# A new order of steps, other engines and fewer zero products ahead of the first expert's fourth chunk, in an attention and mixture-of-experts kernel

## The chip, the cores and the metric

The kernel runs on one core of a Trainium2 chip. The metric is the device time of one execution in microseconds (us). Times before are those of three runs of the unchanged kernel. One execution was also recorded by the hardware profiler; rows quoted below come from that recording. Its engines are PE (matrix products), DVE, ACT and POOL (elementwise work), and SP, which here only issues loads and stores.

## The reference

Queries, keys and values have shape (2 batches, 8 heads, 576 positions, 64). Two attentions are added: one over means of four neighbouring positions, whose output is repeated four times, and one over a band of plus or minus three positions. The sum goes through a mixture of four experts, all of them applied to every token.

```
q_d = q.reshape(B, H, Sd, 4, D).mean(axis=3)      # k_d, v_d alike
out_up = np.repeat(sm_attn(q_d, k_d, v_d), 4, axis=2)
mask = np.abs(pos[:, None] - pos[None, :]) < 4
scores = np.where(mask, scale * q @ k.T, -1e9)
out_local = softmax(scores) @ v
x = (out_up + out_local) as (1152 tokens, 512)
for e in range(4):
    h = np.maximum(x @ w1[e], 0)                  # 512 -> 1024
    out += p[:, e:e+1] * (h @ w2[e])              # 1024 -> 512
```

## The kernel before

The attention is done in four quarters, a0 to a3 (a batch and a half of its positions), and their tokens become the columns of the experts' input, in three chunks of 256 and one of 384. Products of the experts are made from a high and a low part of each operand: `whi` is a weight rounded to the engine's fast type, `wlo` the rest, and `xhi`, `xlo` the same of the tokens.

Every piece of work is a named step. A table, `ENGINE` (L20), gives the engine of steps that may run on several; a list, `ORDER` (L22 to L104), gives one global order of all steps; each engine executes its own steps in that order, whether or not a later one could go first. `WARM` (L21) gives for each step `warmN` a number of 64x64 products of zeros (`warm`, L247), whose result nobody reads. The order stands as written: the scheduler of the framework is switched to manual.

Names of steps up to the first expert: `k00n.0`, `q0n.1`, `v01n.0` and so on load half the heads of keys, queries and values of a batch and half (SP, L259); `a1q.0` to `.3` load the query rows of quarter a1 (L270); `raw101` loads a half of a weight, which is matrix 1 of expert 0, half 1 (L305), and `whi101.0`, `wlo101.0` split it in two parts (L188 or L190, and L321); `vw00` loads a window of values for the band (L291). `k01r.0` copies a loaded half to rows, `k01t.2` transposes it (PE), `k01te.2` evicts it. `k01ds.0` and `.1` sum four neighbouring keys (two additions, L399 and L400), `k01dt` transposes the result, `k01de` evicts it; `v01d.1` sums values (L480, L481). For a quarter: `a0.qt`, `a0.qte`, `a0.qd` prepare the queries (transpose, eviction, sums, L374); `a0.sc2.0` makes local scores (L547), `madd`, `max`, `sub`, `exp`, `sum`, `rec`, `norm` their softmax (max L588, sub L599, norm L618), `blk` transposes 32x32 blocks (L622), `pv` multiplies by the values (L631). `a0.ds`, `dm`, `de`, `da`, `db`, `dq`, `dt`, `dc`, `dv` are the pooled attention in four groups of heads (scores L705, maxima L720, share L750, transposition L758, values L781), and `a0.xd` its eviction. `a0.xs0` adds both for a third of the quarter (L647), `xh0` and `xl0` split the sum into `xhi` and `xlo` (L658). `clear0` and `clear1` zero the block buffers.

`m00` to `m03` are the chunks of expert 0: `m00.m0` is one of eight calls of 12 products (L814: four of `wlo` with `xhi`, four of `whi` with `xhi`, four of `whi` with `xlo`), `m00.r0` and `m00.l0` evict the high part (ACT) and the rest (DVE, L825), `m00.o01` multiplies by a quarter of the second matrix (L839; the first digit is the tile of 128 tokens, the second the part), `m00.g0` evicts (L846). Chunk m00 needs all three thirds of a0. From m03 on come the other experts, whose order is the tail of the same list.

Of the kernel before, what the change touches and what calls it, by code (L numbers as in the profile page):

```python
# [21 lines left out]
ORDER = """  # L22
    warm0 warm37 warm42 warm38 warm43 warm32 warm33 warm45 warm27 warm39 warm29 warm25 warm31 warm23 warm22 warm24
    warm21 k00n.0 k00n.1 q0n.1 q0n.0 k00r.0 q0r.0 q0r.1 warm19 warm2 k00t.0 k00t.1 a0.qt.2 warm3 a0.qt.0 a0.qt.1
    warm20 warm30 warm40 a0.qt.3 k01n.0 v01n.1 k01n.1 kstart0 v01d.1 k01ds.0 k01ds.1 v00n.1 raw101 v00n.0 v01n.0
    raw100 a1q.1 a1q.0 a1q.3 a1q.2 vw00 vw01 mask k00d.1 a0.start clear1 k00d.0 clear0 v00d.0 v00d.1 v01d.0 k00te.1
    k00te.0 k00r.1 a0.qte.0 a0.qte.2 a0.qte.1 k00t.3 warm44 k00t.2 a0.qte.3 k00te.3 k00te.2 a0.qd.0 warm18 a0.sc0.0
    a0.sc0.1 warm1 a0.sc1.0 a0.sc1.1 k01dt k01r.1 a0.qd.1 k00d.3 k01r.0 k01de a0.max1 k01t.1 warm4 k01t.0 k00d.2
    a0.max0 a0.sub1 a0.sub0 k01te.1 a0.ds0 warm16 k01t.2 a0.ds1 a0.dm0 a0.dm1 k01te.0 a0.sc2.0 warm14 warm8 k01t.3
    a0.ds2 a0.exp1 a0.exp0 a0.de0 a0.de1 a0.sum1 k01te.2 a0.da0 a0.da1 a0.db0 a0.sum0 a0.db1 a0.dq0 warm9 a0.dt0  # L30
    a0.ds3 a0.dm3 a0.dm2 a0.rec0 k01te.3 warm15 a0.sc2.1 whi100.1 a0.dc0 a0.dq1 a0.max2 a0.de2 a0.sub2 a0.dt1 warm41
    warm26 a0.norm0 a0.da2 a0.dc1 a0.db2 a0.dq2 a0.de3 a0.exp2 a0.da3 a0.db3 a0.blk0.1 a0.sum2 a0.rec1 a0.rec2
    a0.blk0.0 a0.dq3 a0.norm1 wlo100.1 a0.blk1.0 a0.blk1.1 a0.dv0 warm13 a0.dv1 a0.dt2 warm17 whi101.0 a0.dc2 warm10
    a0.dt3 a1.qt.1 warm34 warm12 a0.dv2 a0.dc3 a0.dv3 a0.pv0 warm28 whi101.1 a0.xd whi100.0 a0.xs0 a0.norm2 a1.qt.0
    a1.start a0.blk2.1 a0.blk2.0 a1.qte.0 warm7 a0.pv1 vw02 warm6 a1.qt.3 warm36 a0.pv2 warm35 a1.qt.2 raw200 a0.xs1
    raw201 praw a0.xh0 a0.xh1 a0.xl0 wlo100.0 a1.qte.1 a1.qte.3 wlo101.0 a0.xs2 whi200.1 a1.qte.2 wlo101.1 a0.xh2
    whi200.0 a1.qd.0 a0.xl1 a1.qd.1 a0.xl2 warm5 a1.sc1.1 warm11 a1.sc2.1 a1.sc2.0 a1.sc0.1 a1.ds0 m00.m0 a1.sc0.0
    m00.m2 m00.m3 a1.ds2 a1.ds1 m00.r0 a1.dm1 a1.madd2 a1.dm0 m00.l0 wlo200.1 a1.de0 a1.de1 a1.da1 a1.da0 a1.db1
    a1.dq1 wlo200.0 a1.db0 whi201.1 a1.dq0 a1.madd0 a1.dm2 a1.max2 a1.dt0 m00.m1 a1.sc1.0 a1.dc0 m00.r3 m00.r2 a1.de2
    a1.dt1 a1.ds3 m00.r1 whi201.0 m00.l3 a1.max0 a1.da2 a1.db2 a1.dm3 m00.l1 k10r.0 k10r.2 k10r.1 k10r.3 a1.dc1 m00.m4  # L40
    k10t.2 a1.dv1 m00.m6 wlo201.1 a1.madd1 a1.sub0 kstart1 a1.sub2 a1.dv0 a1.exp0 a1.de3 a1.exp2 m00.r4 m00.r6 k11r.0
    vw03 k11r.3 k11r.2 v10n.1 k11r.1 vw04 vw05 v11n.1 a1.da3 a1.dq2 a1.dt2 a1.db3 m00.l2 a1.dq3 m00.m5 a1.dc2 a1.dt3
    k10t.1 m00.o00 a1.dv2 k10t.0 m00.m7 m00.r5 a1.dc3 a1.dv3 k10te.2 m00.l4 a1.sum0 wlo201.0 a1.max1 a1.sum2 a1.sub1
    k11t.1 m00.o01 m00.l6 a1.rec0 a1.norm0 a1.blk0.0 a1.blk0.1 gate a1.rec2 a1.norm2 a1.exp1 k10te.0 m00.l5 a1.sum1
    a1.xd k10te.1 a1.pv0 k11te.1 a1.rec1 a1.blk2.1 a1.norm1 m00.r7 a1.xs0 a1.blk1.0 a1.blk1.1 a1.blk2.0 m00.l7 k11t.3
    k11t.0 m00.o10 k11t.2 k10t.3 m00.o02 k11te.0 a1.pv1 a1.pv2 k11te.2 k11te.3 k11d.1 a1.xs1 a1.xh1 k10te.3 a1.xl1
    a1.xs2 a1.xh2 a1.xh0 a1.xl0 a1.xl2 v10n.0 v10d.0 a2.start k10d.0 k10d.1 m00.o11 m00.o03 m00.o12 m00.g0 a2q.2 a2q.1
    a2q.3 a2q.0 a2.qt.0 a2.qt.1 m01.m1 a2.qt.2 a2.qt.3 m01.m0 a2.qte.1 a2.qte.2 a2.qte.0 a2.qd.0 k11d.0 v11d.1
    a2.qte.3 m01.r0 a2.qd.1 m00.o13 a2.ds0 a2.sc2.1 a2.sc0.1 a2.sc0.0 a2.sc1.0 m01.m3 m01.m2 a2.ds2 a2.ds1 m00.g1
    a2.dm1 v11n.0 a3q.3 a2.de1 a2.madd0 a2.dm0 a2.sc1.1 a2.ds3 a2.sc2.0 m01.m6 m01.l0 m01.r1 a2.de0 m01.l1 a2.da0  # L50
    a2.da1 a2.db0 a2.max0 m01.r3 a2.dq0 v10d.1 m01.r2 a2.db1 a2.dq1 a2.dm2 m01.l2 a2.dt0 m01.m4 a2.dt1 a2.madd1
    a2.max1 a2.de2 m01.l3 a2.sub1 v11d.0 vw10 a3q.2 a3q.1 a3q.0 vw11 vw12 m01.r4 a2.madd2 a2.max2 a2.dc0 m01.l4 a2.dm3
    a2.da2 a2.db2 a2.exp1 a2.sub2 a2.dc1 m01.m5 m01.r5 a2.dq2 a2.sub0 m01.l5 m01.r6 a2.de3 m01.l6 a2.sum1 a2.da3
    a2.db3 a3.start a2.dq3 m01.o10 a2.dt2 a3.qt.1 m01.o00 a2.dt3 a2.dv0 a2.dv1 m01.m7 a3.qt.2 m01.o11 m01.o12 a2.rec1
    a2.dc2 a2.exp0 a2.exp2 a2.dc3 a3.qte.1 a2.sum0 a2.rec0 a2.norm1 a2.norm0 a2.blk1.0 a3.qt.0 m01.o01 a2.dv2 a2.dv3
    m01.r7 a2.sum2 a2.blk1.1 a2.blk0.0 a2.rec2 a2.norm2 a3.qte.2 a2.xd a3.qte.0 a2.blk0.1 a2.pv0 m01.l7 a2.blk2.1
    a2.pv1 a2.xs1 a2.blk2.0 a3.qt.3 m01.o02 vw14 vw13 vw15 a3.qte.3 a2.pv2 a3.sc0.1 a3.sc1.0 a3.sc1.1 a2.xh1 a3.qd.0
    a2.xs0 a3.madd1 a2.xh0 a2.xl1 a2.xl0 a3.ds1 m01.o03 m02.m5 m02.m1 a3.ds0 m01.o13 m02.r5 a2.xs2 a3.max1 a3.qd.1
    m01.g0 a3.dm1 a3.dm0 a3.ds3 a3.sc2.0 a3.sc2.1 a3.ds2 a3.sc0.0 m02.m0 m02.m4 a3.sub1 m02.l5 m02.r1 a3.exp1 a3.de1
    m01.g1 a3.da1 a3.db1 a3.dq1 m02.r0 a3.dm2 m02.l0 a3.dt1 a3.de0 a3.madd0 a3.de2 m02.m6 m02.r6 m02.r4 a2.xh2 a3.sum1  # L60
    m02.l1 a3.max0 a3.da2 a3.madd2 a3.db2 a3.da0 a3.dq2 m02.m7 m02.m3 m02.m2 a3.dt2 a2.xl2 a3.sub0 m02.l6 m02.l4
# [1357 lines left out]
```

## Time and profile before

| | us |
|---|---|
| median of three runs | 449.85 (449.63 to 450.29) |
| the profiled execution, its own time | 449.63 |
| its span in the trace | 447.8 |
| PE busy | 439.4 |
| DVE, ACT, POOL busy | 324.5, 207.4, 107.4 |

The span goes from the first to the last recorded instruction; 1.83 us of the execution's own time lie around it. Busy time is the union of an engine's instructions; PE's is that of its products, whose ends are modelled.

### The profile page before, as it was taken

The numbers are of one execution on the slowest core, as the hardware profiler recorded it, in microseconds if no ns is written. First come the engines' busy times: TensorE is split into PE (matmuls) and PEld (weight loads), VectorE is DVE, ScalarE is ACT, GpSimd is POOL, SyncE is SP. The second block draws the span as 40 slices with busy tenths as digits, with TensorE's granted clock in tenths as the row PEclk, the third lists the DMA queues.
The fourth block names the chain that finished last, engine by engine and source line by source line (L and its number), as shares of the span: only waits on it lengthen the run. The fifth ranks groups of instructions, "written<-read, shape, count | busy, mean of one in ns | idle before, by whom it ended". The sixth has DMA issues, their size and how long they took to land.

```text
span 447.8 us, 10468 instructions
## 1 busy us (share of the span) xinstructions
PE 439.4 (98%) x4406; PEld 419.2 (94%) x4406; DVE 324.5 (72%) x574; ACT 207.4 (46%) x395; POOL 107.4 (24%) x129
## 2 busy tenths in 40 slices
...
GB/s 168 235 166 243 160 60 102 103 2 73 1 2 48 1 48 154 142 33 154 59 109 107 124 158 94 2 151 91 93 88 123 156 59 44 49 86 83 21 96 163
DMA packets 69086, 43.12 MB, mean 96 GB/s; under 512 B 27632, under 2 KB 66992, under 8 KB 69040
## 3 DMA queue, kind: packets, MB, share of 16 engines
...
q8 instruction: 34, 0.56, 0.5%
q14 instruction: 12, 0.10, 0.1%
...
## 4 chain that ended last, share of the span: by engine, by line
PE 93%; DVE 3%; DMA 1%; ACT 1%; POOL 0%; issue 0%; SPq 0%; DVEq 0%; POOLq 0%
PE ps L1069 30%; PE ps L1258 26%; PE ps L1271 4%; PE m03h L814 4%; PE m03o L839 4%; PE m01h L814 3%; PE m00h L814 3%; PE m02o L839 3%; PE m02h L814 3%; PE m01o L839 3%; PE m00o L839 3%; PE wps L247 2%; DMA q0n<-in_q_dram 1%; DVE ptb L622 1%; PE a_qt L355 1%; ACT a0pd L728 1%
## 5 line engine op out<-in xcount | busy, mean ns | idle before, releaser
L1258 PE MATMUL ps<-slot,unit 128*128 128x256 f32 x1008 | 119.9, 280 | 1.1 <-DVE unit L1178 1.1
L1258 PEld LDWEIGHTS ps<-slot,unit 128*128 128x128 f32 x1008 | 119.1, 189 | 1.3 <-DVE unit L1178 1.3
L1069 PE MATMUL ps<-xhi,slot 128*128 128x288 f32 x384 | 66.4, 295 | 0.0
L1069 PE MATMUL ps<-xc,slot 128*128 128x288 f32 x432 | 60.4, 295 | 0.0
L1069 PEld LDWEIGHTS ps<-xc,slot 128*128 128x128 f32 x432 | 58.4, 188 | 0.1
L1069 PEld LDWEIGHTS ps<-xhi,slot 128*128 128x128 f32 x384 | 56.2, 188 | 0.0
L1081 ACT ACTIVATE H<-ps 128x288 f32<-128x288 f32 x72 | 27.7, 413 | 56.7 <-PE ps L1069 56.7
L1118 POOL DMA_DIRECT2D raw<-in_moe_w_dram x15 | 19.5, 1331 | 137.6 <-DVE slot L1124 83.3
L1085 DVE TENSOR_TENSOR H<-H,ps 128x288 f32<-128x288 f32 x72 | 29.8, 450 | 20.6 <-PE ps L1069 20.4
L188 ACT CAST slot<-raw 128x1024 fp32r<-128x1024 f32 (+1 forms) x33 | 41.8, 1280 | 0.5 <-DVE raw L1017 0.4
L1023 DVE TENSOR_TENSOR slot<-raw,slot 128x1792 fp32r<-128x1792 f32 x12 | 24.3, 2023 | 23.6 <-PE ps L1069 20.9
L1069 PE MATMUL ps<-xlo,slot 128*128 128x288 f32 x192 | 41.1, 295 | 0.0
L1173 ACT ACTIVATE unit<-H 128x1024 fp32r<-128x1024 f32 x18 | 19.1, 1063 | 28.8 <-PE ps L1258 17.3
L1069 PEld LDWEIGHTS ps<-xlo,slot 128*128 128x128 f32 x192 | 30.7, 188 | 0.0
L1156 DVE SCALAR_TENSOR_TENSOR H<-H 128x1024 f32<-128x1024 f32 (+1 forms) x18 | 28.1, 1576 | 3.5 <-ACT H L1083 3.2
L1169 ACT ACTIVATE unit<-H 128x512 fp32r<-128x512 f32 (+1 forms) x24 | 20.0, 844 | 23.0 <-DVE H L1085 13.4
L1182 DVE SCALAR_TENSOR_TENSOR unit<-H,unit 128x1024 fp32r<-128x1024 f32 x18 | 22.0, 1222 | 7.1 <-ACT unit L1173 7.0
L1124 DVE TENSOR_TENSOR slot<-raw,slot 128x1024 fp32r<-128x1024 f32 x21 | 25.3, 1219 | 2.4 <-ACT slot L188 2.4
L622 DVE STREAM_TRANSPOSE ptb<-pmb 32x256 f32<-32x256 f32 x48 | 20.8, 433 | 5.1 <-PE a1pv L631 2.3
L1178 DVE SCALAR_TENSOR_TENSOR unit<-H,unit 128x512 fp32r<-128x512 f32 (+1 forms) x24 | 22.6, 953 | 1.5 <-ACT unit L1169 1.5
L1280 DVE SCALAR_TENSOR_TENSOR acc<-ps,npr,acc 128x256 f32<-128x256 f32 x48 | 20.7, 477 | 3.3 <-PE ps L1258 3.3
L247 PE MATMUL wps<-wz 128*64 128x64 f32 x286 | 21.8, 234 | 1.0 <-DVE wz L196 1.0
(321 smaller groups left out, 753.8 us busy)
## 6 DMA issues: line engine op xcount, KB each, us to landing
...
```

Source lines behind the costliest of these rows:

```text
L188: nc.scalar.copy(out_, in_)
L247: nc.tensor.matmul(T["wps"][:64, :64], wz, wz, start=True, stop=True)
L622: nc.vector.transpose(ptb[t % 2][32 * j:32 * j + 32, :, :, j, :], T[f"{a}pm{t}"][32 * j:32 * j + 32, :, :, :KW])
L814: nc.tensor.matmul(ps[:, :n], w[:, d, cc:cc + P], x[:, d, n0:n0 + n], start=i == 0, stop=i == len(terms) - 1,)
L839: nc.tensor.matmul(ps[:, cs], T[f"{nm}t{f}"][:, hpart, cc:cc + P], w[:, f % 4, cs], start=f == 0 and x == 0, stop=f == KF - 1 and x == 2,)
L1023: engine(f"wo{e}{i}").tensor_tensor(w1tile(i, 1), raw1(e, i), f32(w1tile(i, 0)), ALU.subtract)
L1069: nc.tensor.matmul(bank(acc_, n, i)[:, :NH // 2], w[:, d * P:(d + 1) * P], x[:, d, n * (NH // 2):(n + 1) * (NH // 2)], start=u == 0 and fi ...
L1081: nc.scalar.mul(dst, at, -1.0)
L1085: nc.vector.tensor_tensor(dst, dst, at, ALU.add)
L1124: engine(f"bo{e}{m}").tensor_tensor(w2tile(m, 1), raw2(q), f32(w2tile(m, 0)), ALU.subtract)
L1156: nc.vector.scalar_tensor_tensor(at[o], at[x], 0.0, at[y], ALU.max, op)
L1258: nc.tensor.matmul(ps[:, t * 256:t * 256 + 256], a[:, f, t * P:t * P + P], b[:, f], start=first_ and (t, f, x) == (0, 0, 0), stop=(t, f, x ...
```

## The change

`ORDER` is new from its start to the step `endattn`, which stands behind the last step of quarter a3; from `endattn` on the list is the same word for word. `ENGINE` gives some 55 steps another engine. Those that matter ahead of chunk m00: the row copies `k00r` and `k01r` go from ACT to DVE; `k01ds.1` and `v01d.1` from POOL to DVE; `clear0`, `a0.dq1` and `a0.norm2` from DVE to POOL; `a0.dq2` from POOL to ACT; `a1.qte.0`, `a0.xh1` and `whi200.1` from DVE to ACT. Behind its start: `whi101.0` goes from ACT to DVE, `wlo101.1` and `wlo200.0` from POOL to DVE, `wlo200.1` and `wlo201.1` from DVE to POOL, and some small steps of a1 to a3 change engine in both directions. `WARM` sums to 110 products where it summed to 143; in both kernels all of them stand ahead of the first product of m00. The zeros at the edge of four value windows become a step of their own, `vw00e` and so on, on DVE or POOL.

```diff
-WARM = [8, 24, 22, 23, 9, 6, 6, 5, 4, 3, 4, 0, 1, 2, 0, 0, 0, 2, 1, 0, 0, 0, 0, 2, 0, 0, 3, 0, 1, 0, 1, 0, 2, 0, 0, 1, 2, 2, 0, 0, 2, 3, 3, 0, 1, 0]
+WARM = [4, 2, 0, 0, 3, 1, 1, 0, 5, 2, 0, 2, 7, 0, 3, 7, 0, 4, 0, 8, 2, 0, 4, 1, 4, 1, 0, 2, 5, 7, 0, 9, 0, 0, 0, 0, 0, 14, 3, 2, 2, 0, 2, 0, 0, 3]
...
     def vwin(b, i):
 
         name = f"vw{b}{i}"
+        first, last = i == 0, i == 2 * NT - 1
+        edge = [f"{name}e"] if first or last else []
+
+        def edges():
+            T[name] = a3.tile([P, H, D], F32, tag="vw", name=name)
+            engine(f"{name}e").memset(T[name][96:128] if last else T[name][0:R], 0.0)
+        if edge:
+            step(f"{name}e", "G", [], edges)
+
         def fn():
-            vw = T[name] = a3.tile([P, H, D], F32, tag="vw", name=name)
-            first, last = i == 0, i == 2 * NT - 1
-            if first:
-                nc.gpsimd.memset(vw[0:R], 0.0)
-            if last:
-                nc.gpsimd.memset(vw[96:128], 0.0)
+            if not edge:
+                T[name] = a3.tile([P, H, D], F32, tag="vw", name=name)
             for j in range(4):
...
-        step(name, "S", [], fn)
+        step(name, "S", edge, fn)
```

What the lists make of the queues is shown at three places. The first is the head of SP's queue. A row is a load, `k01n` a half of the heads of the second half of the keys, `raw_247` the weight half `raw101`, `raw_251` and `raw_463` the half `raw100`. Before:

```order
L259 DMA k00n<-in_k_dram 72x4x256 x2
L259 DMA q0n<-in_q_dram 72x4x256 x2
L259 DMA k01n<-in_k_dram 72x4x256
L259 DMA v01n<-in_v_dram 72x4x256
L259 DMA k01n<-in_k_dram 72x4x256
L259 DMA v00n<-in_v_dram 72x4x256
L305 DMA raw_247<-in_moe_w_dram 128x4x512
L259 DMA v00n<-in_v_dram 72x4x256
L259 DMA v01n<-in_v_dram 72x4x256
L305 DMA raw_251<-in_moe_w_dram 128x4x512
```

Now:

```order
L259 DMA k00n<-in_k_dram 72x4x256 x2
L259 DMA q0n<-in_q_dram 72x4x256 x2
L259 DMA k01n<-in_k_dram 72x4x256 x2
L259 DMA v01n<-in_v_dram 72x4x256
L259 DMA v00n<-in_v_dram 72x4x256
L311 DMA raw_463<-in_moe_w_dram 128x4x512
L259 DMA v01n<-in_v_dram 72x4x256
L270 DMA acc<-in_q_dram 72x8x64
L259 DMA v00n<-in_v_dram 72x4x256
```

The second half of `k01n` moved from the seventh to the sixth place, the values `v01n` behind it, and `raw101` from the ninth place to the 28th, behind the value windows.

The second place is DVE's queue ahead of the first chunk: its last rows up to `a0.xl2`, the last piece of `xlo` that m00 needs. Lines behind L286 stand six higher in the changed kernel (L653 is L647). Before:

```order
L184 TENSOR_SCALAR a1qT<-a_qt_662 128x4x72
L647 TENSOR_TENSOR a0pv_679<-a0pv_679,a0xd 128x384
L190 CAST xhi<-a0pv_679 128x4x96
L647 TENSOR_TENSOR a0pv_706<-a0pv_706,a0xd 128x384
L190 CAST whi_743<-raw_721 128x1024
L374 TENSOR_REDUCE a1qd<-a1qT 128x144
L658 TENSOR_TENSOR xlo<-a0pv_679,xhi 128x4x96
L374 TENSOR_REDUCE a1qd<-a1qT 128x144
L658 TENSOR_TENSOR xlo<-a0pv_706,xhi 128x4x96
```

Now:

```order
L653 TENSOR_TENSOR a0x_652<-a0pv_623,a0xd 128x384
L628 STREAM_TRANSPOSE ptb_92<-pmb_101 32x8x32 x4
L653 TENSOR_TENSOR a0pv_690<-a0pv_690,a0xd 128x384
L380 TENSOR_REDUCE a1qd<-a1qT 128x144
L664 TENSOR_TENSOR xlo<-a0pv_690,xhi 128x4x96
L653 TENSOR_TENSOR a0pv_753<-a0pv_753,a0xd 128x384
L380 TENSOR_REDUCE a1qd<-a1qT 128x144
L726 TENSOR_REDUCE a1dmx<-a1sd_765 72x2
L664 TENSOR_TENSOR xlo<-a0pv_753,xhi 128x4x96
```

The eviction `a1qT`, the cast `xhi` and the cast `whi` of the 1024 columns of `raw_721` are gone from this stretch (they are ACT's now); the maxima `a1dmx` of a1's pooled scores stand ahead of the last `xlo`.

The third place is PE's queue around the first product of m00 (`m00h`). Before:

```order
L631 MATMUL a0pv_706<-ptb_92,vw_688 64x96 x8
L247 MATMUL wps<-wz 64x64
L355 MATMUL a_qt_716<-ident,acc 128x72 x4
L247 MATMUL wps<-wz 64x64 x6
L547 MATMUL a1sl<-kT_231,a1qT 32x32 x64
L705 MATMUL a1sd_828<-kd_232,a1qd 72x144
L705 MATMUL a1sd_829<-kd_232,a1qd 72x144
...
L814 MATMUL m00h_834<-xhi,wlo_589 128x256 x4
L814 MATMUL m00h_834<-xhi,whi_542 128x256 x4
L814 MATMUL m00h_834<-xlo,whi_542 128x256 x4
```

Now:

```order
L247 MATMUL wps<-wz 64x64
L637 MATMUL a0pv_753<-ptb_92,vw_748 64x96 x8
L711 MATMUL a1sd_765<-kd_143,a1qd 72x144
L711 MATMUL a1sd_766<-kd_143,a1qd 72x144
...
L553 MATMUL a1sl<-kT_142,a1qT 32x32 x32
L820 MATMUL m00h_824<-xhi,wlo_740 128x256 x4
L820 MATMUL m00h_824<-xhi,whi_480 128x256 x4
L820 MATMUL m00h_824<-xlo,whi_480 128x256 x4
```

The local scores of a1 (`a1sl`, 16 products for each step) all stand ahead of m00 now, 96 of them, where 64 stood ahead and two steps of 16 behind; the transpositions `a_qt` are earlier, and no zero product stands between the last `a0pv` and m00, where seven stood.

## Rows read from the trace of the kernel before

**Rows 1.** The page: part 1, busy time; part 4, the chain by engine.

```profile
PE 439.4 (98%) x4406; PEld 419.2 (94%) x4406; DVE 324.5 (72%) x574; ACT 207.4 (46%) x395; POOL 107.4 (24%) x129
...
PE 93%; DVE 3%; DMA 1%; ACT 1%; POOL 0%; issue 0%; SPq 0%; DVEq 0%; POOLq 0%
```

**Rows 2.** Busy time by stretch: us, engines (instructions), clock, DMA share, GB/s.

```profile
0.00:42.60 42.60, 39.12 (x806) 34.80 (x806) 26.94 (x80) 23.48 (x47) 27.15 (x44) 1.00 0.82 206
42.60:140.00 97.40, 97.40 (x1275) 84.87 (x1274) 70.45 (x189) 38.35 (x118) 34.61 (x49) 1.00 0.29 61
```

**Rows 3.** The chain of waits, 40.7 to 60 us (start, us, what); timeline of PE.

```profile
40.77 1.25 PE a1sl L547 x78
...
48.68 1.47 PE m00h L814 x12
...
42.60 0.74 PE L814 MATMUL m00h<-xhi,wlo 128*128 128x256 f32 x4
```

**Rows 4.** Busy time of the zero products alone (L247), first stretch.

```profile
0.00:42.60 42.60, 21.84 (x286) 19.60 (x286) 1.00 0.82 206
```

**Rows 5.** Timeline of POOL and ACT: start, us, instruction, [idle before, releaser].

```profile
13.11 1.27 POOL L480 TENSOR_TENSOR v01n<-v01n 72x512 f32<-72x512 f32 x1 [10.82 <-DMA v01n<-in_v_dram]
...
14.76 2.00 ACT L188 COPY kr<-k01n 72x1024 f32<-72x1024 f32 x2 [0.20 <-DMA k01n<-in_k_dram]
...
21.03 0.40 ACT L188 COPY kd<-k01dt 128x288 f32<-128x288 f32 x1 [4.27 <-PE k01dt L405]
```

**Rows 6.** DVE, 20.57 to 43.00 us: busy time, then timeline.

```profile
20.57:43.00 22.43, 19.46 (x58) 1.00 0.78 206
...
20.98 0.45 DVE L382 TENSOR_REDUCE kd<-k00t 128x72 f32<-128x288 f32 x1
...
21.34 0.48 DVE L588 TENSOR_REDUCE a0mx<-a0sl 128x4 f32<-128x128 f32 x2
...
35.56 0.41 DVE L618 TENSOR_TENSOR pmb<-pmb,a0sl 128x256 f32<-128x256 f32 x1
...
37.82 0.67 DVE L184 TENSOR_SCALAR a1qT<-a_qt 128x288 f32<-128x288 f32 x1
...
39.12 0.56 DVE L190 CAST xhi<-a0pv 128x384 fp32r<-128x384 f32 x1
...
40.06 0.68 DVE L190 CAST whi<-raw 128x1024 fp32r<-128x1024 f32 x1
...
42.91 0.45 DVE L720 TENSOR_REDUCE a1dmx<-a1sd 72x2 f32<-72x288 f32 x1
```

**Rows 7.** Groups by line and form, 0 to 140 us: shapes, count, busy us, mean ns.

```profile
L321 POOL TENSOR_TENSOR wlo<-raw,whi 128x256 fp32r<-128x256 f32 x24 | 17.3, 751 | 0.1
...
L374 DVE TENSOR_REDUCE a0qd<-a0qT 128x144 f32<-128x576 f32 x2 | 1.4, 748 | 0.0
...
L618 POOL TENSOR_TENSOR pmb<-pmb,a0sr 128x256 f32<-128x256 f32 x2 | 1.4, 682 | 0.8 <-DVE a0sr L615 0.7
...
L190 DVE COPY kT<-k01t 128x288 f32<-128x288 f32 x2 | 1.3, 665 | 0.0
...
L647 DVE TENSOR_TENSOR a0pv<-a0pv,a0xd 128x384 f32<-128x384 f32 x2 | 1.1, 562 | 0.0
...
L284 POOL MEMSET vw<- 4x512 f32 x2 | 1.0, 516 | 0.0
...
L658 POOL TENSOR_TENSOR xlo<-a0x,xhi 128x384 fp32r<-128x384 f32 x1 | 1.0, 999 | 0.4 <-ACT xhi L188 0.4
```

**Rows 8.** DVE, the 28.10 us from the first expert product.

```profile
42.60:70.70 28.10, 22.07 (x61) 1.00 0.61 125
```

**Rows 9.** Timeline of SP: start and us of a pair of weight loads.

```profile
33.28 1.00 SPq L305 DMA_DIRECT2D raw<-in_moe_w_dram  x2
```

More of the change, by code (lines that the diff above doesn't have):

```diff
@@ L26 @@
[L26 to L60, printed above, removed]
@@ L61 @@
-    m02.l1 a3.max0 a3.da2 a3.madd2 a3.db2 a3.da0 a3.dq2 m02.m7 m02.m3 m02.m2 a3.dt2 a2.xl2 a3.sub0 m02.l6 m02.l4
-    a3.exp0 m02.r3 a3.rec1 m02.l3 m02.r2 a3.dc2 a3.dc1 a3.db0 a3.dm3 a3.sum0 m02.l2 m02.o00 m02.o01 a3.dq0 a3.de3
-    a3.da3 a3.db3 a3.dq3 a3.dt3 m02.o02 a3.dv2 m02.r7 a3.rec0 m02.l7 a3.dv1 m02.o10 a3.dt0 m02.o03 a3.max2 a3.sub2
-    a3.exp2 a3.norm0 a3.norm1 a3.sum2 a3.blk0.0 a3.blk0.1 a3.pv0 a3.dc3 a3.dc0 a3.rec2 a3.norm2 a3.blk1.0 a3.blk1.1
-    a3.dv0 a3.dv3 a3.blk2.0 a3.blk2.1 m02.o11 a3.pv2 a3.pv1 a3.xd a3.xs0 a3.xs1 m02.g0 a3.xs2 a3.xh1 a3.xh0 a3.xh2
@@ L101 @@
[L101 to L103 removed]
+    warm25 mask warm12 a0.start warm17 kstart0 warm29 k00n.0 k00r.0 warm31 k00t.1 k00t.0 k00te.1 k00n.1 warm45 q0n.0
+    warm19 warm9 k00r.1 k00t.2 k00te.0 q0n.1 k00t.3 k00d.0 k00d.2 warm40 k01n.1 warm28 warm42 q0r.0 k00d.1 k00d.3
@@ new lines @@
+    warm27 k01n.0 v01n.0 warm34 k01ds.0 warm39 k00te.2 q0r.1 a0.qt.2 k00te.3 a0.qt.0 v01d.0 a0.qte.2 k01r.1 a0.qt.1
+    warm15 a0.qte.0 k01ds.1 k01r.0 a0.qt.3 k01t.3 k01te.3 a0.qte.1 a0.sc0.0 a0.qd.0 a0.qte.3 a0.sc0.1 a0.max0 k01t.1
+    a0.sub0 a0.qd.1 k01t.0 k01te.0 k01te.1 k01dt k01de a0.sc1.0 a0.sc1.1 a0.ds0 a0.ds1 a0.max1 v00n.0 v00d.0 warm24
+    a0.dm0 a0.exp0 a0.sum0 a0.rec0 a0.norm0 a0.sub1 warm8 clear0 a0.de0 a0.dm1 a0.de1 k01t.2 a0.sc2.0 k01te.2 a0.da0
+    a0.sc2.1 a0.db0 a0.dq0 a0.da1 raw100 a0.max2 a0.db1 a0.dq1 a0.sub2 a0.exp1 v01n.1 a0.ds2 whi100.1 a0.ds3 a0.dm3
@@ new lines @@
+    a1.qte.0 a1.sc1.1 a1.sc1.0 wlo100.1 a0.xs1 a0.xh1 warm6 vw02 a0.pv2 a0.xl0 a1.qd.0 a1.ds0 warm7 wlo100.0 a0.xl1
+    a0.xs2 a1.sc0.0 a1.qd.1 a1.dm0 a0.xh2 a0.xl2 a1.sc2.0 raw101 k10r.3 a1.madd0 whi101.0 whi101.1 wlo101.1 m00.m2
+    m00.r2 a1.ds1 a1.dm1 m00.l2 a1.de0 a1.max0 m00.m0 a1.sub0 a1.da0 a1.db0 a1.ds2 warm21 a2.start a1.de1 m00.r0
+    m00.l0 m00.m1 k10r.0 raw200 m00.r1 a1.madd2 wlo101.0 k10r.2 a1.exp0 a1.sum0 a1.rec0 a1.dq0 a1.dm2 a1.da1 whi200.0
+    a1.db1 a1.dq1 a1.ds3 a1.de2 m00.m3 m00.l1 k11r.1 a1.dt0 k10r.1 m00.r3 m00.m4 a1.dt1 a1.dc1 a1.madd1 a1.dm3 a1.de3
```

115 lines of the change are left out of this document (72 added, 43 removed).

## The prediction

> **What bounds the kernel now.** I read the page first: PE is busy 439.4 of 447.8 us, and of the chain that ended last 93% is PE's [rows 1]. Such a share is a mean, and PE is kept busy by products of zeros too; so the next view is busy time by stretch, cut where the first product of chunk m00 starts, at 42.60 [rows 2, 3]. Behind the cut PE is busy in all of 97.40 us, and no zero product runs there any more. Ahead of it PE is busy 39.12 of 42.60 us, but 21.84 of these are zeros [rows 2, 4]. The reader is to see two regimes: up to 42.60 PE waits for attention a0 and fills the time; from there it is the bound without a gap, with a fixed amount of work, while DVE is busy 70.45 of 97.40. Since the order from the last step of a3 on is the old one, the time changes by three things alone: how much earlier m00 starts, what work goes from one side of the cut to the other, and what new waits PE gets behind it.
>
> Ahead of the cut it is DVE that paces. Its row from the maxima of a0 to the last `xlo` takes from 20.57 to 43.00, 22.43 us with 19.46 busy [rows 6]; the row starts late because the pooled keys are late. The last half of `k01` is taken up at 14.76 [rows 5]; POOL sums both halves after `v01d.1`, and the summed keys reach `kd` at 21.03, 6.3 us later [rows 5].
>
> **The start of DVE's row.** In the new order the last half of `k01` is the sixth load. The sixth load before was the half of `v01` that POOL took up at 13.11 [rows 5], so I put it there, 1.65 earlier than 14.76. Its sums are split: one half on POOL, the other, which lands earlier, on DVE. The instruction at 13.11 took 1.27, and a half sum is that and one of half its columns: 1.27 + 0.64 = 1.9 us. The pooled keys are summed at 13.1 + 1.9 = 15.0, against 21.03 for `kd` before, and their scores need not hold anybody up. From 13.1 DVE does, in its order, a row copy (0.68, as the copy of 1024 columns in [rows 6]), `k01te.3` (0.67) and both sums of a0's queries (0.75 each) [rows 7], and `max0` with `sub0` (0.48 for each pair [rows 6]): 13.1 + 0.68 + 0.67 + 1.50 + 0.96 = 16.9.
>
> **The length of DVE's row.** What follows up to `a0.xl2` is the old row with eight steps out and three in. Out, from [rows 6]: one pooled key sum 0.45; `max0` and `sub0` 0.48 each (they are in the 16.9); `norm2` 0.41 and `dq1`, taken at the same 0.41; `a1.qte.0` 0.67; `xh1` 0.56; `whi200.1` 0.68. Sum 4.14. In: the window's zeros `vw00e`, on POOL 0.52 [rows 7] and taken at that; a1's first maxima 0.45 [rows 6]; and `v01d.1`, which no row shows on DVE. Its bounds are POOL's 1.9 above, and from DVE's `xs`, 0.562 for 384 columns [rows 7], 0.562 x 768/384 = 1.12 for its 512 and 256; I take the DVE one, since engine and operation are the same. Sum 2.09. The row keeps its waits: 22.43 - 4.14 + 2.09 = 20.4, and it ends at 16.9 + 20.4 = 37.3. Before, the first product of m00 stood 0.40 ahead of that end (42.60 against 43.00), because eight products come ahead of the first that reads `xlo`. So m00 would start at 36.9 by DVE.
>
> What would keep the moved steps from being free is named here. ACT takes `a1.qte.0`, `xh1` and `whi200.1` and gives away four row copies; it is busy 23.48 of 42.60 [rows 2]. POOL takes two `clear` and shares: from 13.1 it does four half sums (7.6), six steps like `norm` (0.68 each, 4.1), two clears of 1024 columns (twice the 0.516 of a 512 memset, 2.1), eight pieces of `wlo` (0.751 each, 6.0) and one `xlo` (1.0) [rows 7]. That is 20.8, so it has `wlo100.0` by 33.9 if it never waits, 3.0 in hand. The two rows, DVE's and POOL's, end near each other, and each waits for the other's products, so I take 37.2 for the start, 5.4 earlier. The bounds: with none of DVE's 2.97 of waits 33.9 (POOL's row says the same), with twice as many 39.9.
>
> **Fewer zero products.** 33 of 143 go; one costs 21.84/143 = 0.153 us [rows 4], so PE has 33 x 0.153 = 5.0 us less ahead of m00. Were they not gone, an earlier start would not be possible; as they are, PE's work ahead of the cut is 39.12 - 5.0 + 0.6 (below) = 34.7 in 37.2 us, 2.5 idle where 3.48 were. The granted clock is 1.00, the 2.4 GHz level, in both stretches [rows 2], and by this row nothing changes in it. The Trainium skill, "TensorE: Matmul & The Clock Gate", section "HAM oscillation — how this bites in real kernels", speaks against the change: it says that a wait between groups of products can throttle the engine again, which then starts the next group at half speed. No stretch of this trace shows that; the sum goes by the row, and the rule is a rival below.
>
> **Moved over the cut.** The four calls of local scores of a1 ahead of m00 took 1.25 us, 0.31 each [rows 3]; two more now stand ahead. PE has 0.6 us less behind it: -0.6.
>
> **New waits behind the cut.** DVE gets, net of what goes both ways, some 1.8 us more behind the cut: `whi101.0` 0.68, three `norm` or `sub` of 0.41, a cast, and evictions of a1 in both directions; the two `wlo` pieces only change places with two others. 70.45 + 1.8 = 72.3 in 96.8: 24.5 idle instead of 27.0. In all that is enough, so what counts is the places. I added durations along each engine's new row from the start of m00. DVE has `wlo200.0` after 9.5 us, and PE reads it in m00.o10 at 10.8; POOL has `wlo200.1` after 11.6 (it waits for `whi200.1` on ACT), needed in m00.o01 at 14.2; DVE has m00.l7 after 26.2, needed in m00.o13 at 28.1. The same addition over DVE's old row gives 21.6 where 22.43 passed, 4% less; stretched so, 0.9 remains in hand at each of the two DVE places. That is little for rows that wait for each other. I take 0.6 lost at each, 1.2 in all; the bounds are 0 and, with the additions stretched by 15%, 0.1 at o10, 2.0 at o13 and some 0.9 behind it at a2's pooled values (`v10d.1` stands on DVE behind an eviction and a sum there): 3.0. The split of the window's zeros changes nothing else: they take a step of 0.52 out of POOL or put it there, ahead of the windows' loads, in both kernels.
>
> **The sum.** -5.4 - 0.6 + 1.2 = -4.8. The profiled execution took 449.63, so 444.8; it lies 0.22 below the median of the three runs, so **445.1** against 449.85.
>
> **Rivals.**
> - *m00 starts as DVE's row says, and nothing waits behind it*: 449.85 - 5.7 - 0.6 = 443.5. For it: PE has no wait in 97.40 us before. Against: 0.9 in hand is thin. Chance 0.10.
> - *POOL sets the start.* Its 3.0 in hand are used up when it waits 5 us for denominators and casts: start at 38.9, 449.85 - 3.7 - 0.6 + 1.2 = 446.8. Chance 0.07.
> - *DVE becomes the bound behind the cut*, up to m00.l7. In the 28.10 us after the first product it was busy 22.07, 79% [rows 8]. Waits of 3.0 to 6.9 there give 446.9 to 450.8; chance 0.12, of which 0.05 from waits of 5.1 on, within 0.2% of before. It **ends slower** if PE loses over 6.9 (5.4 + 0.6 + 0.9), when 26.2 us of DVE's row take 28.1 + 6.9 = 35.0, a share of 75%. For: DVE's steps now wait for ACT and POOL at more places. Against: 79% with fewer steps crammed in. A loss of 7.2 gives 451.1; chance 0.05.
> - *The clock falls* in a gap of PE ahead of m00 or beside it, the page's rule above. An m call takes 1.47 us [rows 3]; at 1.2 GHz it would take 2.94, and four slow calls lose 5.9: 451.0. By the granted clock of before, 1.00 throughout, I give it 0.05 (0.03 slower, 0.02 the same).
> - *`raw101` comes late.* It is the 28th load now, and DVE stops at `whi101.0`, with m00.l2 queued behind it and `wlo101.1`; PE's fourth m call waits for that. By the additions this costs from a landing at 38.9 on. The nearest row is the weight pair issued at 33.28, the 29th and 30th load of before [rows 9], whose second use stands at 40.06 [rows 6]: at worst 40.1, so 1.2 us, 446.3; the gain is gone only at 43.7. Chance 0.03, of which 0.01 slower.
> - *The forecast* keeps 0.58.
>
> **How the numbers follow.** A change under 0.2% (0.9 us) can't be told from none with these runs. Faster: 0.58 + 0.10 + 0.07 + 0.07 of DVE's case + 0.02 of the late load = 0.84. The same: 0.05 + 0.02 = 0.07. Slower: 0.05 + 0.03 + 0.01 = 0.09. The forecast's own bounds are a start at 36.2 to 38.6 with stalls of 0 to 3.0, not all at one end: 443.2 to 447.5. The range goes from 443.0 to 448.8: below lies little of the no-stall case (0.03), above what ends the same or slower (0.16).
>
> **What would show each step.** Right: m00 starts near 37 us; the summed keys reach `kd` near 16; zero products take near 17 us; the granted clock stays 1.00; PE's waits behind the start sum to 1 us, before m00.o10, m00.o13 or a2's pooled values; from the tail on every stretch is as long as before. Wrong: a start after 39 (POOL's or DVE's row waits more), waits of over 3 us on DVE or POOL behind the cut, or a granted clock under 1.00.

## The result and the profile after

The changed kernel takes 447.15 us, the median of 20 executions (441.31 to 450.03), against 449.60 for the kernel before (448.36 to 450.29, 20 executions): 2.45 us less, 0.54%. The ratio, 0.9905 with a 95% interval of 0.9879 to 0.9930 (0.95%, 4.3 us of 449.6), leaves out the seven slowest executions of the changed kernel, from 448.31 on, and none of the kernel before. On another chip, with all twelve executions of the changed kernel in it, the ratio was 0.9941 (e5), so a gain of 0.5 to 0.6% is the safer figure. The forecast was 445.1 in 443.0 to 448.8.

The spread is news: 8.7 us where the kernel before has 1.9. It goes with TensorE's granted clock. The five executions with a mean clock of 1.000 took 442.45 to 444.38 and the one with 0.999 441.31, those with 0.996 445.21 to 449.09, those with 0.992 447.91 to 449.70, the ones with 0.989 and 0.983 449.24 and 450.03.

The profiled execution took 445.98, its span is 444.1 and its mean clock 0.996. From the page, PE's busy time, the queue called instruction, and the chain by engine [rows 1]:

```profile
PE 434.0 (98%) x4340; PEld 416.0 (94%) x4340; DVE 329.6 (74%) x580; ACT 206.6 (47%) x398; POOL 101.9 (23%) x122
...
q8 instruction: 34, 0.56, 0.5%
...
PE 97%; issue 1%; DVE 1%; ACT 0%; DVEq 0%
```

Busy time of the two stretches, cut at the first products of m00 and m03 (columns as in [rows 2]), and the zero products alone:

```profile
0.00:38.91 38.91, 34.56 (x804) 30.99 (x804) 29.26 (x81) 20.23 (x47) 22.80 (x38) 0.99 0.82 208
38.91:136.42 97.51, 96.40 (x1215) 85.25 (x1209) 76.08 (x196) 40.87 (x122) 33.86 (x47) 0.98 0.34 74
```

```profile
0.00:38.91 38.91, 16.92 (x220) 15.39 (x220) 0.99 0.82 208
```

The start of m00 moved from 42.60 to 38.91 (-3.69); from there to m03 it is 97.51 where it was 97.23 (+0.28); the rest of the span is 307.68 where it was 307.97 (-0.29). Sum -3.70. The zeros take 16.92 us [rows 4], as forecast. So nearly all of the gain is the start, and it is smaller than the 5.4 of the forecast. PE's waits show why (engine, line, releaser: us, times, longest; those for the first `wz` and, far behind m03, for `unit` are left out):

```profile
PE a0pv L637 <- issue: 2.1, 1, 2.1
...
PE m01h L820 <- issue: 1.1, 1, 1.1
...
PE a0sl L553 <- issue: 0.6, 1, 0.6
PE wps L247 <- issue: 0.5, 1, 0.5
```

These four lines are new in kind: 2.1 us ahead of a product of `a0pv`, 1.1 in `m01h`, 0.6 in `a0sl`, 0.5 at a zero product, each put down to "issue", which is to say that no semaphore explains it. Ahead of m00 the list has no wait of PE for another engine once its first zero product has started: of 38.91 - 34.56 = 4.35 us idle, 1.0 lies ahead of that product and 3.2 in three of these stops. PE's timeline shows where the longest is:

```profile
34.33 0.59 PE L637 MATMUL a0pv<-ptb,vw 128*64 128x96 f32 x9
37.03 0.55 PE L637 MATMUL a0pv<-ptb,vw 128*64 128x96 f32 x7 [2.11 <-issue]
...
38.91 1.22 PE L820 MATMUL m00h<-xhi,wlo 128*128 128x256 f32 x4
...
41.64 0.74 PE L820 MATMUL m00h<-xhi,wlo 128*128 128x256 f32 x4
```

The stop lies in the middle of one step, the third `pv`, whose data were all there for its first nine records. Behind it the first call of m00 takes 2.73 us (38.91 to 41.64) instead of 1.47 [rows 3]. The clock, by stretch of PE (busy, clock, DMA share, GB/s):

```profile
34.92:37.03 2.11, 0.00 (x1) 1.00 0.96 340
38.00:39.00 1.00, 1.00 (x69) 0.71 1.00 185
39.00:41.00 2.00, 2.00 (x10) 0.50 0.94 120
41.00:42.00 1.00, 1.00 (x7) 0.58 0.91 306
```

PE did nothing for 2.11 us. Some 1.4 us after it resumed the granted clock fell to 0.50, the 1.2 GHz level: a mean of 0.71 over 38 to 39 puts the fall near 38.4, 0.58 over 41 to 42 the rise near 41.8, 3.4 us in all. What PE had executed at each stop is the count in its busy time from the start:

```profile
0.00:14.90 14.90, 13.27 (x221) 1.00 0.79 197
...
0.00:25.60 25.60, 23.50 (x474) 1.00 0.83 195
...
0.00:36.90 36.90, 32.69 (x725) 1.00 0.81 205
...
0.00:82.30 82.30, 76.94 (x1355) 0.98 0.65 153
```

221, 474, 725, 1355: the differences 253, 251 and 630 are, within one record, 2, 2 and 5 times 126. A block of 126 recorded products is 252 recorded instructions with their weight loads. The page's queue "instruction" moved 34 packets of 16 KB, and PE executed 4340 + 4340 instructions, 255 for each packet. One such packet starts between 34.25 and 34.50, just ahead of the long stop (queue: packets, MB, their time as a share of 16 engines' 0.25 us):

```profile
q8 instruction: 1, 0.02, 29.8%
```

It takes 0.298 x 16 x 0.25 = 1.19 us, so it has landed by 35.7, and PE goes on at 37.03. In the packet records of the kept traces the same holds at all 21 stops of this kind: the packet ends 1.3 to 1.7 us before PE goes on. By the same count the kernel before passed a block about as fast, 41.2 to 44.7, and did not stop. There the packet started between 42.25 and 42.50, some 1.2 us after the border; here it started some 3.5 us after (border at 30.97). The DMA engines were less loaded there from the border on, 0.71 against 1.01 (columns as in [rows 2]), before and now:

```profile
41.20:44.70 3.50, 3.50 (x147) 3.10 (x139) 2.15 (x5) 1.12 (x2) 3.50 (x6) 1.00 0.71 131
```

```profile
30.97:34.49 3.52, 3.52 (x139) 3.29 (x132) 3.38 (x8) 2.15 (x4) 3.52 (x6) 1.00 1.01 333
```

The Trainium skill, "Runtime: NRT & Kernel Launch", section "Instruction fetch mechanics", says that an engine's instructions stream in by blocks of 16 KiB, 256 instructions, the next one while the current one is executed, and that this is mostly hidden. The count agrees; hidden it is not here.

The engines that the forecast spoke of, ACT, DVE and POOL (timelines), and DVE over 28.10 us from m00's first product [rows 8]:

```profile
16.14 0.44 ACT L188 COPY kd<-k01dt 128x288 f32<-128x288 f32 x1
...
22.61 0.62 DVE L486 TENSOR_TENSOR v01n<-v01n 72x512 f32<-72x512 f32 x1
...
23.26 1.37 DVE L487 TENSOR_TENSOR vd<-v01n 72x256 f32<-72x256 f32 x1
...
37.62 0.57 DVE L653 TENSOR_TENSOR a0pv<-a0pv,a0xd 128x384 f32<-128x384 f32 x1 [2.68 <-PE a0pv L637]
...
33.11 2.78 POOL L327 TENSOR_TENSOR wlo<-raw,whi 128x256 fp32r<-128x256 f32 x4
```

```profile
38.91:67.01 28.10, 22.83 (x60) 0.95 0.48 105
```

The summed keys are in `kd` from 16.14 (21.03 before [rows 5]). `v01d.1` takes 0.62 and 1.37 on DVE beside POOL's sums, 2.0 in all where 1.12 was taken. DVE has its second `xs` at 33.12 and then waits 2.68 for the stopped PE. POOL ends `wlo100.0` at 35.9. With the 2.1 us simply taken off, m00 would start at 36.8, an estimate; the forecast took 37.2.

### The profile page after: what moved, and what is told of

The parts are those of the page before. It is cut to its first block, busy times and chain, and to the rows that moved or that the text cites. A ratio compares the mean times of both kernels' runs of the same rounds, so it can differ in the third digit from the quotient of the medians.

```text
span 444.1 us, 10352 instructions
## 1 busy us (share of the span) xinstructions
PE 434.0 (98%) x4340; PEld 416.0 (94%) x4340; DVE 329.6 (74%) x580; ACT 206.6 (47%) x398; POOL 101.9 (23%) x122
## 4 chain that ended last, share of the span: by engine, by line
PE 97%; issue 1%; DVE 1%; ACT 0%; DVEq 0%
PE ps L1075 30%; PE ps L1264 27%; PE ps L1277 4%; PE m03h L820 4%; PE m03o L845 4%; PE wps L247 3%; PE m00h L820 3%; PE m01h L820 3%; PE m02h L820 3%; PE m00o L845 3%; PE m01o L845 3%; PE m02o L845 3%; PE a_qt L361 1%; PE a0pv L637 1%; DVE slot L1130 1%
## 5 line engine op out<-in xcount | busy, mean ns | idle before, releaser
L1124 POOL DMA_DIRECT2D raw<-in_moe_w_dram x15 | 19.5, 1297 | 145.5 <-DVE slot L1130 85.2
L188 ACT CAST slot<-raw 128x1024 fp32r<-128x1024 f32 (+1 forms) x33 | 41.8, 1280 | 0.5 <-DVE raw L1023 0.4
L1017 POOL DMA_DIRECT2D raw<-in_moe_w_dram x8 | 11.8, 1532 | 36.5 <-DVE H L1091 20.7
```

The costliest lines, as they stand in the source:

```text
L188: nc.scalar.copy(out_, in_)
```

## The experiments

Theory A: PE stops at the border of a block of its own instructions when the next block has not come, because the new order packs short products (a1's scores) into one block while loads are busy; a long stop lets the clock fall. Theory B: PE waits for data. Theory C: fewer zeros as such let the clock fall. The first four runs shared a chip on which the kernel before itself took 448.41 to 460.98 in 23 executions with clocks of 0.972 to 1.00; there the verdicts rest on the profiles. On the chips of the later sets it took 448.36 to 450.51, but for one of 46 executions.

**Fewer zeros at the start (e1).**

```diff
-WARM[31] = 9
+WARM[31] = 3
```

> The changed kernel with 6 zero products fewer in its first group, ahead of 6 us; nothing else. Theory A (PE stops where a block of its own instructions, 126 recorded products long, has not come in yet, and the clock falls after a long stop): all stops move with the count. The one behind 725 recorded products leaves the middle of the third a0pv and lies 12 recorded products later, in a1sd; the block ahead of it takes some 4.5 us instead of 3.9, so the stop shrinks from 2.1 to about 1.5 us; the one behind 1355, 1.1 us in m01h, goes. Time about 444 to 445. Theory B (PE waits there for data, the loaded window or another engine): the stop stays ahead of the same product of a0pv with the same 2 us, the time stays at 446. Theory C (fewer zeros as such let the clock fall): six more gone, the clock is granted 0.996 or less, 446 or more.

447.27 us median of 6 (444.01 to 452.71), ratio 0.9864 (0.9784 to 0.9944). PE's timeline:

```profile
34.68 0.47 PE L711 MATMUL a1sd<-kd,a1qd 64*72 64x144 f32 x4
36.99 0.63 PE L711 MATMUL a1sd<-kd,a1qd 64*72 64x144 f32 x4 [1.84 <-issue]
```

The stop now lies 12 records later in the program, in `a1sd`, and the trace has 724 products ahead of it; the third `pv` runs through. It shrank from 2.11 to 1.84 (1.5 forecast), that in `m01h` is gone. m00 starts at 38.37. B falls: a wait for the window would have stayed where it was. C is not parted by this run: the mean clock is 0.996 or less in all six executions, but this chip's clock falls with the kernel before too.

**Thirty-six zeros fewer at the start (e2).**

```diff
-WARM[12], WARM[19], WARM[28], WARM[29], WARM[31] = 7, 8, 5, 7, 9
+WARM[12], WARM[19], WARM[28], WARM[29], WARM[31] = 0, 0, 0, 0, 0
```

> The changed kernel with 36 zero products fewer, all from the groups ahead of 9 us, where PE waits for loads. Theory A: the blocks' borders fall 72 recorded products later in the program, on stretches where PE runs through a block fastest: behind 671 (3.3 us for the block before it), 797 (2.9), 1301 (1.2, the local scores of a2) and 1679 (2.4, those of a3). Stops of 1.5 to 4 us at several of these counts, several falls of the clock, and a time of 449 to 456 although only idle fill was taken out. Theory B: stops at the same products as before, time 446 within 1 us. Theory C: the clock falls in the first 15 us, where the zeros are gone, and m00 starts as it did; 446 to 448.

458.59 us (6; 455.61 to 464.62), ratio 1.0142 (1.0072 to 1.0212). The counts of the expectation are those of the program's places in the old numbering; less the 72 records taken out they are 599, 725, 1229 and 1607. Timeline and counts:

```profile
36.80 0.58 PE L553 MATMUL a1sl<-kT,a1qT 64*32 64x32 f32 x44 [2.40 <-issue]
...
43.48 0.33 PE L553 MATMUL a1sl<-kT,a1qT 64*32 64x32 f32 x8 [3.13 <-issue]
...
87.70 0.53 PE L553 MATMUL a2sl<-kT,a2qT 64*32 64x32 f32 x37 [3.29 <-issue]
...
0.00:34.50 34.50, 28.56 (x598) 1.00 0.84 188
...
0.00:40.50 40.50, 32.12 (x724) 0.97 0.86 199
...
0.00:85.00 85.00, 73.05 (x1227) 0.94 0.63 142
```

Three stops of 2.4 to 3.3 us stand at 598, 724 and 1227 records, all inside local scores; none shows at 1607. The profiled execution took 455.61, that of e1 on the same chip 444.01, though only 30 more zeros at the start are gone: each of these borders now meets a run of short products. A holds at its sharpest place. Not all of the loss is theirs: with the zeros of the start gone, the eight records of transpositions from 5.75 and from 8.14 take 1.19 and 1.22 us, where the changed kernel's take 0.72 each, which A does not explain.

**Three score steps behind the first m calls (e3).**

```diff
-... a1.sc1.1 a1.sc1.0 ... a1.sc2.0 ... m00.m2 ... m00.m0 ...
+... m00.m2 ... m00.m0 a1.sc1.1 a1.sc1.0 a1.sc2.0 ...
```

> The changed kernel with three of a1's six score steps (sc1.1, sc1.0, sc2.0, 96 recorded products) moved behind the first two m calls of m00; the same work. Theory A: the block that ends at 725 recorded products is filled by longer products, takes 6 us or more, and PE has no stop ahead of m00; m00 starts near 36 instead of 38.9, the clock stays 1.00 there, time 442 to 443.5, less spread. Theory B: the stop of 2 us in the third a0pv stays, m00 starts 1.2 us earlier only by the work moved behind it, which comes back there: 446. Theory C: the clock falls as before, 446.

```profile
36.19 0.72 PE L820 MATMUL m00h<-xhi,wlo 128*128 128x256 f32 x4
```

m00 starts at 36.19, at the full clock, with no stop ahead of it, and the profiled execution, at 1.00 throughout, took 444.89, above the 442 to 443.5 of theory A: stops of 0.8 and 1.0 came at later borders, and 0.9 for DVE at the moved scores. The median of 12 is 453.48, ratio 1.0003 (0.9943 to 1.0062), on the restless chip; as a time it decides nothing.

**The kernel before with as many zeros fewer as in the change (e4).**

```diff
-WARM[1], WARM[2], WARM[3] = 24, 22, 23
+WARM[1], WARM[2], WARM[3] = 13, 11, 12
```

> The kernel before with 33 of its 143 zero products taken out of its three largest groups, as many as the change takes out; no other edit. Theory A: the zeros cost nothing by themselves, but the borders of blocks fall 66 recorded products later: one at 791, in or behind the local scores of a1, with 1.5 to 2.5 us for the block before it, so PE stops there for 2 to 4 us just ahead of m00 and the clock falls: 452 to 455. The reading of the prediction (zeros are fill, DVE paces up to m00): no change, 449 to 450, no stop. Theory C: the clock falls between 9 and 20 us, where the zeros are gone; 450 to 451. A rival to the prediction (zeros stand in the way of real work): 446 to 448.

454.22 us (12; 451.20 to 459.97), ratio 1.0044 (1.0003 to 1.0085). Clock by stretch of PE:

```profile
8.00:12.00 4.00, 3.03 (x26) 0.60 1.10 233
...
29.00:33.00 4.00, 4.00 (x45) 0.54 0.70 132
...
33.00:39.00 6.00, 6.00 (x61) 0.50 0.99 340
```

Here C has its part. PE stops 1.9 us for a load's copy ahead of 9 us and 1.4 for POOL ahead of 28, and behind each the clock is at half; m00 starts at 46.62, 4.0 later than before, with a stop at a border of only 0.8 ahead of it (2 to 4 expected by A). The zeros of the old order were not mere fill.

**The changed kernel again (e5).** No edit.

> The changed kernel unedited, beside the others of this set on one chip. Theory A (PE stops at borders of 126 recorded products when the next block of instructions has not come): stops behind 725 recorded products again, of 1 to 3 us, m00 near 38 to 39, perhaps behind 221, 473 and 1355; times that go with the granted clock, some 444 at 1.00 and 2 to 4 us more for each fall. Theory B (a wait for data): the stop may be anywhere or missing.

446.80 us (12; 444.34 to 448.30), ratio 0.9941 (0.9924 to 0.9959). The stop behind 725 records came again in the third `pv`, now of 3.6 us; m00 started at 42.11 in that profile, which took 448.21. Of 29 executions of the kernel before in this set 28 had a clock of 0.998 or more; of the 12 of the changed kernel two.

**Both helpful edits (e6).** The edit of e1, and of e3's three steps only sc1.1 and sc1.0.

> The changed kernel with both edits that helped: 6 zero products fewer in the first group, and two of a1's score steps (sc1.1, sc1.0, 64 recorded products) behind the first two m calls of m00. Theory A: no stop ahead of m00 over 0.5 us, m00 starts near 36, none behind 1355; clock 1.00; the profiled run at 441 to 442.5, its median at or under that of the changed kernel beside it. If the gain of the moved scores comes back behind m00, as it did in part with three moved: 443 to 444.

444.23 us (6; 441.41 to 445.12), ratio 0.9881 (0.9854 to 0.9908) beside the 0.9941 of e5 on the same chip. PE's timeline:

```profile
36.12 0.25 PE L553 MATMUL a1sl<-kT,a1qT 64*32 64x32 f32 x4 [0.90 <-issue]
36.31 0.74 PE L820 MATMUL m00h<-xhi,wlo 128*128 128x256 f32 x4
```

A stop of 0.9 is left, still behind 724 records, not under 0.5; m00 starts at 36.31, m03 at 132.62 (136.42), and the profiled execution took 442.19 at a clock of 1.00. Four of the six executions still had 0.995 or 0.996.

**Five steps back on DVE (e7).**

```diff
-'a0.dq1': 'G', 'a0.norm2': 'G', 'clear0': 'G', 'a1.qte.0': 'A', 'a0.xh1': 'A'
+'a0.dq1': 'V', 'a0.norm2': 'V', 'clear0': 'V', 'a1.qte.0': 'V', 'a0.xh1': 'V'
```

> The changed kernel with five steps ahead of m00 back on DVE, where the kernel before had them: dq1 and norm2 of a0, clear0, a1.qte.0 and a0.xh1, together 0.41 + 0.41 + 0.9 + 0.67 + 0.56 = 3.0 us. The prediction's reading (DVE's row sets the start of m00): the start moves from 38.9 to 39.9 to 42, since 2 of the 3 us may lie under the stop for instructions; 447 to 449. Rival (the row of PE or POOL sets it, DVE has room): start within 0.5 of 38.9, 445 to 447.

449.35 us (10; 446.98 to 450.77), ratio 0.9998 (0.9980 to 1.0016).

```profile
39.77 0.91 PE L637 MATMUL a0pv<-ptb,vw 128*64 128x96 f32 x7 [2.56 <-issue]
...
42.60 1.22 PE L820 MATMUL m00h<-xhi,wlo 128*128 128x256 f32 x4
```

The start moves by 3.69 to 42.60 for 3.0 us of steps, beyond the forecast 42. Of the 3.69, 2.29 come ahead of the stop, which begins at 37.21 instead of 34.92: PE has waits of 0.9, 0.7 and 0.6 for DVE there that the changed kernel's profile does not show. The stop is 0.45 longer and hides nothing, and behind it PE needs 2.83 us to m00 instead of 1.88, at half clock. So DVE's row had some 0.7 us of room in that profile, no more, and this relief alone, undone, takes the whole gain.

**The keys' part undone (e8).**

```diff
-'k01ds.1': 'V', 'k01r.0': 'V', 'k01r.1': 'V'
+'k01ds.1': 'G', 'k01r.0': 'A', 'k01r.1': 'A'
```

> The changed kernel with the keys' part undone: k01ds.1 back on POOL (2.0 us there for 1.1 on DVE), the row copies k01r.0 and .1 back on ACT (1.05 each for 0.69). The loads keep their new order. The prediction's reading (DVE's row paces, the pooled keys only have to come before its first maxima at 18): pooled keys 2 us later, start of m00 0 to 1 us later, 446 to 447. Rival (the early pooled keys carry the gain): start 2 us later or more, 448.

449.25 us (10; 448.27 to 452.73), ratio 1.0008 (0.9988 to 1.0028). Timeline and clock of PE:

```profile
18.82 0.50 PE L411 MATMUL k01dt<-ident,k01dp 72*128 72x72 f32 x2 [2.45 <-POOL k01dp L406]
...
18.00:25.00 7.00, 6.18 (x101) 0.51 1.01 182
...
43.30 0.75 PE L820 MATMUL m00h<-xhi,wlo 128*128 128x256 f32 x4
```

My own expectation falls, the rival's 2 us are exceeded. The sum stands behind `v01d.0` in POOL's row; PE waits 2.45 us for it in `k01dt`, the clock is 0.51 from 18 to 25 and at half again from 35.1 to 38.5, and m00 starts at 43.30, although no stop stands at 725 records here. The early keys matter because PE stands in `k01dt`: DVE then waits 3.25 us for the local scores behind it.

**One load moved (e9).** On SP, vw03 right behind raw101 (`raw101 vw03` in `ORDER`).

> The changed kernel with one load step moved on SP: the fourth value window vw03, whose buffer comes free at the first a0pv, stands right behind raw101, so the key rows k10r and the weights raw200 and raw201 are issued some 2 us later. PE's rows are untouched. Theory A2 (the block of instructions comes late because it stands behind those loads): the stop behind 725 recorded products shrinks from 2.1 to 3.6 us to under 1.5, the clock falls less, 444 to 445. Rival (the block is late because PE runs through the one ahead of it in 3.9 us, whatever the loads do): the stop stays at 2 to 3.6 us, 446 to 447.

443.80 us (4; 443.06 to 444.03), ratio 0.9877 (0.9861 to 0.9894). SP's issue of raw200 in the changed kernel, and that of the key rows and raw200 in this one, with PE's third `pv`:

```profile
30.21 1.29 SPq L311 DMA_DIRECT2D raw<-in_moe_w_dram  x1
```

```profile
33.13 1.28 SPq L270 DMA_DIRECT2D acc<-in_k_dram  x2
...
34.46 1.87 SPq L311 DMA_DIRECT2D raw<-in_moe_w_dram  x1
...
36.48 0.55 PE L637 MATMUL a0pv<-ptb,vw 128*64 128x96 f32 x7 [0.25 <-issue]
```

With raw200 issued 4.25 us later (34.46 for 30.21) the stop at the same place is 0.25 us. So whether PE has to wait for a block depends on the traffic, not only on how short the block ahead of it is. In this profile PE ran at half clock from 29.7 to 33.1, so that block also took longer (31.69 to 35.98, 4.3 us instead of 3.7). The packet parts the two: it starts between 34.00 and 34.25 here, 2.3 to 2.6 us after the border, against some 3.5 in the changed kernel. So the block came sooner, and that does not hang on PE's pace. All four executions have clocks of 0.996 or more. What lies ahead of the half clock is no long stop (timeline, then the stretch at half clock):

```profile
26.84 1.02 PE L764 MATMUL a0pdt<-ident,a0pd 72*72 72x72 f32 x8 [0.62 <-ACT a0pd L753]
```

```profile
29.71:33.12 3.41, 3.41 (x94) 0.50 0.82 226
```

**All three edits (e10).**

> The three edits together: 6 zeros fewer in the first group, two score steps of a1 behind the first m calls, vw03 ahead of the key rows. Theory A2: no stop over 0.5 us ahead of m00, clock 1.00 in most executions, 441 to 443. Rival: as with the first two edits, a stop of about 0.9 us, 442 to 445.

442.53 us (4; 441.95 to 444.07), ratio 0.9848 (0.9829 to 0.9866): a median under those of both kernels; the changed kernel itself was not run on this chip. Three of four executions ran at 1.00 (441.95 to 442.64); the profiled one, 444.07, had half clock from 29.6 to 33.1, and m00 started at 37.58 with no stop behind 724 records ahead of it.

**The keys' part alone in the kernel before (e11).** Loads `k01n.1 k01n.0 v01n.1`, k01ds.1 and k01r on DVE, k01dt behind warm1.

> The kernel before with the keys' part of the change alone: both halves of k01 are loaded ahead of the values, one half is summed on DVE, the row copies k01r are on DVE, and the transposition k01dt stands behind the 24 zeros of warm1 rather than behind two score steps; all other rows are the old ones. If the early pooled keys carry the gain (undone in the changed kernel, they cost 4.4 us up to m00): m00 starts 2 to 4 us earlier, 446 to 448. If the rest of DVE's and PE's rows sets the start: within 1 us, 449 to 450.

449.76 us (12; 449.05 to 450.58), ratio 1.0013 (1.0003 to 1.0024).

```profile
42.20 0.75 PE L814 MATMUL m00h<-xhi,wlo 128*128 128x256 f32 x4
```

m00 starts 0.4 earlier, at 42.20, and no time is won. But the edit did not make the keys early. ACT, and DVE's row copy (timelines):

```profile
19.59 0.40 ACT L188 COPY kd<-k01dt 128x288 f32<-128x288 f32 x1 [5.68 <-PE k01dt L405]
...
15.52 2.59 DVE L190 COPY kr<-k01n 72x1024 f32<-72x1024 f32 x1
```

The summed keys reach `kd` at 19.59, only 1.4 us earlier than before, since the row copy takes 2.59 us and `k01ds.1` follows it on DVE; DVE's maxima of a0 start at 20.71, where they started at 20.57. So whether keys as early as the changed kernel's (16.14) would help the old order is not tested.

## Why the prediction was right

**The start.** That DVE's row is long enough to set the start held: 3.0 us more on it move PE's arrival at the stop by 2.3 (e7). That it alone paces did not: in the changed kernel's profile PE, with its zeros, waits for no other engine ahead of m00, so the two rows are about equally long. Without the stop m00 would start at 36.8, by 36.9 for DVE and 37.2 taken. That is in part luck, for terms were off and cancelled: `v01d.1` cost 2.0 for 1.12 and the row copy `k01r.0` 1.79 for 0.68, while the row's waits were shorter. POOL's 3.0 in hand were enough. That early keys "need not hold anybody up" is true of the split as made; e8 shows that their absence does, through PE.

**The zeros.** 16.92 us against 16.8. But "by this row nothing changes in it" (the clock) failed. The same cut in the old order costs 4.0 us up to m00 by stops that let the clock fall (e4), and in the new one the mean clock was 0.996 or less in 14 of 20 executions. The rival of the falling clock, at 0.05, came true in kind: smaller in size (1.26 us in m00's first call instead of 5.9), and not in outcome. By the prediction's own list a granted clock under 1.00 is a sign of being wrong. The rule of the Trainium skill, "TensorE: Matmul & The Clock Gate", section "HAM oscillation — how this bites in real kernels", that a wait may throttle the engine, which no row of before could show, agrees with these traces in part: half clock follows the 2.11 us here, 2.45 in e8 and 1.9 and 1.4 in e4. The next products do not start at half speed here, as the rule has it, but 1.4 us pass first. No fall follows the 1.1 in `m01h` or the 0.9 of e6, and three falls (29.7 in e9, 29.6 in e10, 35.1 in e8) stand 2.8 us behind a wait of only 0.6 for ACT, which in e1 and e3 has none behind it. What decides is open.

**What failed** is the step that PE only waits for other engines. No term, no rival and no row was given to its own instructions: 2.11 us ahead of m00 and 1.1 in `m01h`. A row was there, 34 packets in the queue "instruction" on the page of before, and that a block is 126 products could have been worked out from it. That the new order runs through one in 3.7 us (30.97 to 34.67 in the trace of after) would not have been enough, since the old one did so in 3.5 without a stop; the loads at that moment had to be read too.

**New waits behind the start.** 1.2 us were taken at m00.o10 and m00.o13, up to 3.0 with a2's values: none of these stopped PE, though DVE was busy 22.83 of 28.10 us instead of 22.07. In their place came the 1.1 in `m01h` and the 1.26 of the slow clock, 2.4 in sum.

**Moved work.** Two score steps, -0.6. With +2.4 the stretch should be 97.23 + 1.8 = 99.0; it is 97.5. Some 1.5 us of PE's time are gone that no moved step accounts for: the same 144 products of the second matrix keep PE busy 36.80 us instead of 37.67, the pooled scores 3.71 instead of 4.17. e9, at the full clock behind its start (134.34 - 38.29 = 96.05, with one stop of 0.9), has them too. That PE changes less often between kinds of products is a guess; it stays open.

**The sum.** -4.8 forecast; -3.65 in the profiled execution, -4.3 by the ratio, -2.45 by the medians of all. That the time lies in the range is luck in part: the start came 1.7 us later than forecast, behind it 2.4 of other losses took the place of the 1.2, and 1.5 us that nobody forecast made up for most of the difference. raw101 was in time: DVE's `whi101.0` ran at 39.91 without a wait.
